# Attention and two expert layers on one core: values of two neighbouring head pairs in one group of matmuls

## The chip, the cores and the metric

The kernel runs on one core of a Trainium2 chip. The metric is the time of one execution in microseconds (us) of device time, as the median of several runs. The core has a matmul engine (PE, TensorE), whose weight loads the profile lists apart (PEld), a vector engine (DVE), an activation engine (ACT), GpSimd (POOL), and queues that issue DMAs (SP above all). Each engine works through its own list of instructions in order and waits on semaphores of the others.

## The reference, cut to what matters

Attention over 4 batches, 8 heads, 576 positions and head size 64, with a bias that depends on the two positions; its output, as 2304 tokens of 512, goes through a two-layer network (w_in to 2048, w_out back), and then through one of eight experts for each token.

```python
scores = scale * np.matmul(q, k.transpose(0, 1, 3, 2)) + bias
attn = np.exp(scores - max); attn = attn / (sum + 1e-9)
out = np.matmul(attn, v)                      # the products of this change
x = out.transpose(0, 2, 1, 3).reshape(2304, 512)
h = x @ w_in; g = np.maximum(0.01 * h, h)     # x @ w_in is the filler of attention
x = g @ w_out                                 # and then the experts
```

## The kernel before, in words

The program has three parts. The first, `phase1`, makes the bias table, does attention, and beside it already multiplies attention's output by w_in. The second multiplies by w_out and chooses experts, the third is the experts. The change touches the first alone.

Attention goes through 4 batches `b`; each batch is cut by query rows into two halves, `hf` 0 with 256 rows and `hf` 1 with 320 (`HALVES`); in each half four head pairs `p` follow each other. One (b, hf, p) is a group, of two steps in the first half and three in the second; a step is one block of 128 query rows (64 for the last block of a batch) for both heads of the pair. In a step `n` the program emits, in this order: the transposes of the step's probabilities (`transposes`, PE tiles `pst` and `psx`, copied by DVE or ACT to `pth` and `ptt`), the scores of step n+2 (`scores`, tile `pss`, two PSUM banks in turn; DVE adds the bias and takes the minimum, line 421), exponentials (`exps`, ACT), the normalisation of step n+1, small jobs (splits of q and k, loads), and units of the filler.

Numbers are carried in two parts, high and low, so that most products are three matmuls. The filler (`Filler`, `up_units`, line 528, tile `psh`) is x times w_in for the half that was finished before: 16 units of 12 matmuls each. `Filler.run(ns)` adds to a debt and hands out units while it is positive; `quota` is what a step adds, one half of it in the middle of the step and one at its end. Step 7 drains the filler.

At the last step of a group `values` multiplies the transposed probabilities of all its rows by the values: ten matmuls, two heads side by side in the columns of the array (each writes 64 of the 128 output partitions), five blocks of positions, into one bank `psv` of the pool `psM`, which the filler's `psh` shares and which has two banks. The profile counts each of these ten as two. In the next step `x_split` (through `values_out`) lets DVE copy the bank to x's high part (a CAST, line 78) and form the low part (line 82). After the fourth pair of a half, x times w_in of that half is added to the filler.

The order in which instructions stand on an engine isn't the order of this code: a scheduler places them, each engine's list being fixed when the program is built. The lines `tile_position=(0, 64 * h)` make the array work as two column tiles in `values`; scores, transposes and the filler use it whole.

## Time and profile before

| | us |
|---|---|
| median of three runs | 1012.41 (1012.28 to 1012.85) |
| the profiled execution, own time | 1009.6 |
| its span, first to last instruction | 1007.7 |
| PE busy in the span | 971.8 |
| DVE busy | 676.5 |
| ACT busy | 546.6 |
| matmuls of `values` begin, first and last | 60.0 and 504.2 |

The profiled execution is one run; what lies between its span and its own time is start and end outside the instructions. Attention with its filler ends at about 505 us, the last filler units at about 533 us. Busy PE includes the time in which a matmul's modelled end overlaps the next start, so starts are more telling than busy shares.

### The profile page before, as it was taken

The numbers are of one execution on the slowest core, as the hardware profiler recorded it, in microseconds if no ns is written. First come the engines' busy times: TensorE is split into PE (matmuls) and PEld (weight loads), VectorE is DVE, ScalarE is ACT, GpSimd is POOL, SyncE is SP. The second block draws the span as 40 slices with busy tenths as digits, with TensorE's granted clock in tenths as the row PEclk, the third lists the DMA queues.
The fourth block names the chain that finished last, engine by engine and source line by source line (L and its number), as shares of the span: only waits on it lengthen the run. The fifth ranks groups of instructions, "written<-read, shape, count | busy, mean of one in ns | idle before, by whom it ended". The sixth has DMA issues, their size and how long they took to land.

```text
span 1007.7 us, 19031 instructions
## 1 busy us (share of the span) xinstructions
PE 971.8 (96%) x6294; PEld 804.4 (80%) x6294; DVE 676.5 (67%) x1712; ACT 546.6 (54%) x1102; POOL 76.8 (8%) x85
## 2 busy tenths in 40 slices
PE   5999999999999999999998999999999999999996
PEld 2455878888899889998897888888877888888884
DVE  8999999889855677668676866579893355313312
ACT  6799787556756676656454333343562455424422
POOL 0023230000000000000000000001001111111110
PEclk9999999999999999999999999999999999999998
DMA  7898898999754576546187433437405257312410
GB/s 239 259 274 258 271 314 288 308 298 292 238 158 137 170 226 187 160 121 177 54 282 218 145 106 113 128 105 256 121 21 220 73 203 257 122 46 95 161 43 24
DMA packets 137600, 180.62 MB, mean 179 GB/s; under 512 B 19841, under 2 KB 89857, under 8 KB 137362
## 3 DMA queue, kind: packets, MB, share of 16 engines
q1 hardware_dynamic: 115554, 149.83, 48.5%
q10 hardware_dynamic: 18576, 18.97, 5.3%
q0 software_dynamic: 3360, 10.49, 3.1%
q8 instruction: 52, 0.85, 0.4%
q14 instruction: 58, 0.48, 0.2%
HBM read 196.65 MB, written 43.94 MB: 239 GB/s over the span
## 4 chain that ended last, share of the span: by engine, by line
PE 60%; issue 19%; DMA 11%; DVE 5%; ACT 2%; POOL 1%; SPq 1%; POOLq 0%; ACTq 0%; DVEq 0%
PE psx L787 19%; PE psh L528 16%; PE pss L416 7%; PE psv L503 7%; PE pst L467 5%; DMA out_dram<-o,sidx 5%; DMA wo_raw<-in_w_out_dram 3%; PE psb L272 3%; DMA w_raw<-in_w_in_dram 1%; POOL xg L1244 1%; DVE prob L421 1%; PE psx L489 1%; DMA prob<-bias 1%; DMA kraw<-in_k_dram 1%; DVE mk L230 1%
## 5 line engine op out<-in xcount | busy, mean ns | idle before, releaser
L528 PE MATMUL psh<-x,wi 128*128 128x256 f32 (+1 forms) x1536 | 224.7, 297 | 0.0
L528 PEld LDWEIGHTS psh<-x,wi 128*128 128x128 f32 x1536 | 211.0, 189 | 0.6 <-issue 0.5
L429 ACT ACTIVATE prob<-prob,stat 128x576 f32<-128x576 f32 x144 | 111.3, 773 | 66.4 <-DVE stat L421 56.8
L421 DVE CUSTOM_DVE_ANT_0 prob<-pss,prob 128x576 f32<-128x576 f32 x144 | 108.0, 751 | 20.4 <-PE pss L416 15.8
L787 PE MATMUL psx<-woh,gh 128*128 128x512 f32 x288 | 112.9, 392 | 0.0
L787 PE MATMUL psx<-wol,gh 128*128 128x512 f32 x288 | 112.6, 391 | 0.0
L787 PE MATMUL psx<-woh,gl 128*128 128x512 f32 x288 | 112.3, 390 | 0.0
L82 DVE TENSOR_TENSOR htl<-pt,hth 128x512 fp32r<-128x512 f32 x40 | 25.8, 686 | 124.8 <-ACT hth L70 124.0
L70 ACT ACTIVATE gh<-g 128x512 fp32r<-128x512 f32 x72 | 45.3, 631 | 112.7 <-PE psx L787 91.7
L467 PE MATMUL pst<-ident,prob 128*128 128x128 f32 x576 | 88.7, 278 | 4.3 <-DVE pth L78 2.1
L467 PEld LDWEIGHTS pst<-ident,prob 128*128 128x128 f32 x576 | 65.5, 140 | 24.4 <-issue 12.5
L416 PE MATMUL pss<-kt,qhi 128*128 128x288 f32 x256 | 81.0, 332 | 0.9 <-DVE kt L82 0.5
L416 PE MATMUL pss<-kt,qlo 128*128 128x288 f32 x256 | 72.3, 297 | 0.0
L503 PE MATMUL psv<-pth,vs 128*64 128x256 f32 (+1 forms) x512 | 71.6, 412 | 0.0
L1244 POOL DMA_INDIRECT xg<-x,gidx x22 | 23.4, 1063 | 615.2 <-DMA ws<-in_mw_dram 545.8
L804 DVE SCALAR_TENSOR_TENSOR junk<-x1s,en 128x512 bf16<-128x512 f32 x96 | 66.0, 688 | 1.1
L82 DVE TENSOR_TENSOR gl<-g,gh 128x512 fp32r<-128x512 f32 x72 | 49.3, 688 | 24.7 <-ACT gh L70 21.5
L1275 PE MATMUL pu<-w1h,xh 128*128 128x512 f32 x160 | 65.0, 406 | 0.3 <-ACT xh L70 0.3
L272 PE MATMUL psb<-mk,coef 128*32 128x79 f32 (+48 forms) x640 | 54.0, 411 | 11.6 <-DVE mk L230 9.8
L1275 PE MATMUL pu<-w1l,xh 128*128 128x512 f32 x160 | 63.3, 396 | 0.0
L1306 PE MATMUL pd<-w2h,hth 128*128 128x512 f32 x160 | 62.6, 391 | 0.7 <-ACT hth L70 0.7
L1275 PE MATMUL pu<-w1h,xl 128*128 128x512 f32 x160 | 63.3, 396 | 0.0
(223 smaller groups left out, 1833.5 us busy)
## 6 DMA issues: line engine op xcount, KB each, us to landing
ws<-in_mw_dram SPq DMA_DIRECT2D x164, 512.0 KB
prob<-bias SPq DMA_DIRECT2D x64, 288.0 KB
g<-h SPq DMA_DIRECT2D x72, 256.0 KB
prob<-bias SPq DMA_DIRECT2D x64, 256.0 KB
bias<-bt SPq DMA_DIRECT2D x36, 295.5 KB
h<-hst ACTq DMA_DIRECT2D x64, 160.0 KB
w_raw<-in_w_in_dram SPq DMA_DIRECT2D x16, 512.0 KB
h<-hst ACTq DMA_DIRECT2D x64, 128.0 KB
```

The lines of the kernel that those rows point to most:

```text
L82: nc.vector.tensor_tensor(out=out, in0=x, in1=hi.bitcast(F32), op=ALU.subtract)
L272: nc.tensor.matmul(ps[32 * q:32 * q + 32, :b - a], lhsT=e.coef.rearrange("p g h -> p (g h)"), rhs=x, start=True, stop=True, tile_position= ...
L416: nc.tensor.matmul(ps[:, jh, :288], lhsT=lhsT, rhs=kt[:, c0 + 288 * jh:][:, :288], start=(k == 0), stop=(k == len(ops) - 1),)
L421: nc.vector.tensor_tensor_reduce(out=prv, in0=ps[:, :, :288], in1=prv, scale=-0.125, scalar=3.0e38, op0=ALU.add, op1=ALU.min, accum_out=st ...
L429: nc.scalar.activation(out=pr[:, h], in_=pr[:, h], func=AF.Exp, bias=stat[:, 0, h:h + 1], scale=-1.0, accum_out=stat[:, 1, h:h + 1],)
L467: nc.tensor.transpose(ps[:, 128 * c:128 * c + 128], pr[:, h, 64 * h + 128 * c:][:, :128], e.ident)
L503: nc.tensor.matmul(ps[64 * h:64 * h + 64, :n], lhsT=vs[:, c, h], rhs=ph[:, h, c, :n] if c < 4 else pt[:, :n], start=(c == 0), stop=(c == 4 ...
L528: nc.tensor.matmul(ps[:, :n], lhsT=w[:, kc], rhs=x[:, kc, :n], start=(k == 0), stop=(k == 3 * KD - 1),)
L787: nc.tensor.matmul(ps, lhsT=a[:, c % 4], rhs=w[:, c], start=(k == 0), stop=(k == 3 * KF - 1))
L804: nc.vector.scalar_tensor_tensor(out=junk, in0=x1, scalar=1.0, in1=e.en[:, k], op0=ALU.mult, op1=ALU.mult, accum_out=e.dots[:, t, k:k + 1],)
L1275: nc.tensor.matmul(ps, lhsT=a[:, k], rhs=w[:, k, c], start=(i == 0), stop=(i == 3 * KD - 1))
L1306: nc.tensor.matmul(ps, lhsT=a[:, k], rhs=w[:, k], start=(k == 0 and j == 0), stop=(k == 7 and j == 2))
```

## The change

The products of pairs 0 and 1 are made together at the last step of pair 1, and those of pairs 2 and 3 at the last step of pair 3: 20 matmuls in a row where there were two times ten. For that the transposed probabilities of a pair are kept until its neighbour's are there (`pth` and `ptt` get two buffers, `pts` collects them). In the first half both results (2 x 256 columns) go to one PSUM bank, and `x_split` copies both with one CAST and one subtraction of 512 columns; in the second (320 columns) each has a bank, so that both banks of `psM` are taken for a while. `quota` grows by the estimated time `pv` of one pair's values for each pair, spread over the steps, and `fl.debt -= pv` takes as much away at the step in which a joined group stands; at step 8, three quarters of one for the group of the drained step 7. Over a half, what is added and what is taken are equal (2 `pv`).

```diff
--- before.py
+++ after.py
@@ -301,7 +301,7 @@
         self.nc, self.e = nc, e
         self.kv, self.v, self.qs, self.prob, self.ps = {}, {}, {}, {}, {}
         self.raw, self.qraw = {}, {}
-        self.pt = None
+        self.pt, self.pts = None, []
         self.free = list(range(PROBS))
         self.slot = {}
 
@@ -452,9 +452,10 @@
     def new_group(self):
         e = self.e
         self.pt = (
-            e.ptp.tile([128, 2, 4, 320], F32, tag="pth", name="pth", bufs=1),
-            e.ptp.tile([128, 320], F32, tag="ptt", name="ptt", bufs=1),
+            e.ptp.tile([128, 2, 4, 320], F32, tag="pth", name="pth", bufs=2),
+            e.ptp.tile([128, 320], F32, tag="ptt", name="ptt", bufs=2),
         )
+        self.pts.append(self.pt)
 
     def transposes(self, st, h):
         nc, e = self.nc, self.e
@@ -492,25 +493,38 @@
 
 
     def values(self, g):
+
         nc, e = self.nc, self.e
         b, hf, p = g
         n = HALVES[hf][1]
-        vs = self.v[b, p]
-        ph, pt = self.pt
-        self.psv = ps = e.psM.tile([128, 512], F32, tag="m", name="psv")
-        for c in range(5):
-            for h in range(2):
-                nc.tensor.matmul(
-                    ps[64 * h:64 * h + 64, :n], lhsT=vs[:, c, h], rhs=ph[:, h, c, :n] if c < 4 else pt[:, :n],
-                    start=(c == 0), stop=(c == 4), tile_position=(0, 64 * h),
-                )
+        tile = lambda: e.psM.tile([128, 512], F32, tag="m", name="psv")
+        if hf == 0:
+            self.psbank = ps = tile()
+            self.psv = [ps[:, n * k:n * k + n] for k in range(2)]
+        else:
+            self.psv = [tile()[:, :n] for k in range(2)]
+        for k, (ph, pt) in enumerate(self.pts):
+            vs = self.v[b, p - 1 + k]
+            for c in range(5):
+                for h in range(2):
+                    nc.tensor.matmul(
+                        self.psv[k][64 * h:64 * h + 64], lhsT=vs[:, c, h],
+                        rhs=ph[:, h, c, :n] if c < 4 else pt[:, :n],
+                        start=(c == 0), stop=(c == 4), tile_position=(0, 64 * h),
+                    )
+        self.pts = []
 
     def x_split(self, g, xh, xl):
         nc = self.nc
         b, hf, p = g
         n = HALVES[hf][1]
-        COPY[X_HI[b]](nc, xh[:, p, :n], self.psv[:, :n])
-        lo_dve(nc, xl[:, p, :n], self.psv[:, :n], xh[:, p, :n])
+        if hf == 0:
+            parts = [(slice(p - 1, p + 1), self.psbank[:, :2 * n].rearrange("p (k i) -> p k i", k=2))]
+        else:
+            parts = [(p - 1 + k, self.psv[k]) for k in range(2)]
+        for q, ps in parts:
+            COPY[X_HI[b]](nc, xh[:, q, :n], ps)
+            lo_dve(nc, xl[:, q, :n], ps, xh[:, q, :n])
 
 
 def up_units(nc, e, b, hf, xh, xl):
@@ -652,7 +666,7 @@
         if prev is None:
             return
         pb, ph, pp = prev
-        if pp == 0:
+        if pp == 1:
             pool = e.xp if ph == 0 else e.late
             xs = [pool.tile([128, KD, HALVES[ph][1]], F32R, tag=f"x{i}{ph}", name=f"x{i}", bufs=1) for i in range(2)]
         at.x_split(prev, *xs)
@@ -667,6 +681,8 @@
         last = st[3] == HALVES[hf][2][-1]
 
         quota = 40 * 800.0 / 6.5 if n < 8 else KF * 1600.0 / 8 if hf == 0 else (13 if b == 0 else 17) * 1280.0 / 12
+        pv = 20 * HALVES[hf][1] if n >= 8 else 0.0
+        quota += 2 * pv / (8 if hf == 0 else 12)
         nx = steps[n + 2] if n + 2 < ns else None
         while loaded < ns and at.free:
             at.load_bias(steps[loaded])
@@ -693,6 +709,10 @@
         if n == 7:
             fl.drain()
         else:
+            if last and p % 2:
+                fl.debt -= pv
+            if n == 8:
+                fl.debt -= 0.75 * pv
             fl.run(quota / 2)
         if nx and nx[3] != 4:
             at.exps(nx, 1)
@@ -703,8 +723,9 @@
                 e.late = ctx.enter_context(tc.tile_pool(name="late", bufs=1, side="left"))
                 e.wi.append(new_w_in(e.late))
                 at.free.append(PROBS)
-            at.values(g)
-            prev = g
+            if p % 2:
+                at.values(g)
+                prev = g
     at.x_split(prev, *xs)
     fl.add(up_units(nc, e, prev[0], prev[1], *xs))
     return fl
```

How the lists of instructions move, at three places. PE, second half of the third batch, first head pair, before: the last filler matmuls, ten matmuls of values, then the next step's transposes and scores.

```order
L528 MATMUL psh<-x_4047,wi_77 128x256
L528 MATMUL psh<-x_4046,wi_78 128x256
L503 MATMUL psv<-pth,vs 64x320 x8
L503 MATMUL psv<-ptt,vs 64x320 x2
L467 MATMUL pst<-ident,prob 128x128 x4
L489 MATMUL psx<-ident,prob 128x128
L416 MATMUL pss<-kt,qtail 128x288 x8
L467 MATMUL pst<-ident,prob 128x128 x4
L528 MATMUL psh<-x_4046,wi_77 128x256
```

After, the same half with pairs 0 and 1:

```order
L416 MATMUL pss<-kt,qhi 128x288
L416 MATMUL pss<-kt,qlo 128x288
L510 MATMUL psv<-pth,vs 64x320 x8
L510 MATMUL psv<-ptt,vs 64x320 x2
L510 MATMUL psv<-pth,vs 64x320 x8
L510 MATMUL psv<-ptt,vs 64x320 x2
L468 MATMUL pst<-ident,prob 128x128 x4
L490 MATMUL psx<-ident,prob 128x128
L416 MATMUL pss<-kt,qtail 128x288 x8
L468 MATMUL pst<-ident,prob 128x128 x8
L416 MATMUL pss<-kt,qhi 128x288
```

Two groups have become one without anything between them; the filler no longer follows the next step's second transposes but comes later, and the transposes of two steps stand together.

DVE at the same places, from the normalisation (line 445) to the reduction of scores (line 421), before:

```order
L445 TENSOR_SCALAR prob<-prob,stat 128x576
L78 CAST x_4755<-psv 128x320
L78 COPY pth<-pst 128x4x128
L82 TENSOR_TENSOR x_4756<-psv,x_4755 128x320
L78 COPY ptt<-psx 128x128
L421 ISA prob,stat<-pss,prob 128x576
```

After:

```order
L445 TENSOR_SCALAR prob<-prob,stat 128x576
L78 CAST x_4937<-psv 128x320
L82 TENSOR_TENSOR x_4938<-psv,x_4937 128x320
L78 CAST x_4937<-psv 128x320
L78 COPY pth<-pst 128x4x128
L82 TENSOR_TENSOR x_4938<-psv,x_4937 128x320
L78 COPY ptt<-psx 128x128
L421 ISA prob,stat<-pss,prob 128x576
```

The first pair's CAST and subtraction stand ahead of the second pair's CAST, and that ahead of the copy of transposed probabilities (`pth`).

PE, first half of the first batch, pairs 2 and 3 (step 7), after:

```order
L416 MATMUL pss<-kt,qlo 128x288
L510 MATMUL psv<-pth,vs 64x256 x2
L468 MATMUL pst<-ident,prob 128x128 x4
L416 MATMUL pss<-kt,qhi 128x288
L416 MATMUL pss<-kt,qlo 128x288
L416 MATMUL pss<-kt,qhi 128x288
L416 MATMUL pss<-kt,qlo 128x288
L510 MATMUL psv<-pth,vs 64x256
L510 MATMUL psv<-ptt,vs 64x256 x2
L510 MATMUL psv<-pth,vs 64x256 x8
L510 MATMUL psv<-ptt,vs 64x256 x2
L468 MATMUL pst<-ident,prob 128x128 x4
```

Here the scheduler has put other work into the joined group: two matmuls and the last thirteen stand in these rows in two pieces, and one and four more stand in two pieces ahead of them; the other fifteen joined groups are whole.

## Rows read from the trace of the kernel before

**Rows 1.** Windows: stretches of the span; busy us of each engine, TensorE clock, DMA share, GB/s.

```profile
0.00:107.00 107.00, 93.50 (x921) 50.59 (x922) 97.18 (x242) 86.73 (x181) 18.83 (x27) 1.00 0.84 255
107.00:148.00 41.00, 39.80 (x310) 33.89 (x309) 37.42 (x93) 32.37 (x85) 13.04 (x15) 1.00 0.96 306
148.00:246.00 98.00, 92.87 (x698) 84.09 (x699) 86.48 (x216) 60.26 (x136) 1.48 (x1) 1.00 0.92 298
246.00:504.60 258.60, 257.91 (x1995) 229.59 (x1993) 181.78 (x507) 159.60 (x355) 0.00 (x0) 1.00 0.55 165
```

**Rows 2.** Chain of waits, shares by line, of 148 to 246 us, then 246 to 504.6.

```profile
by line: DMA wo_raw<-in_w_out_dram 34.9%; PE psh L528 9.1%; DMA w_raw<-in_w_in_dram 5.7%; issue 5.1%; PE pss L416 4.9%; DVE wo_t L107 4.8%; DVE prob L421 4.8%; DVE wo_t L103 4.2%; PE pst L467 3.4%; DMA prob<-bias 3.2%; PE psv L503 2.9%; DVE
...
by line: PE psh L528 43.8%; PE psv L503 18.1%; PE pss L416 17.2%; PE pst L467 14.2%; PE psx L489 1.7%; DMA prob<-bias 1.2%; issue 0.8%; ACT prob L429 0.7%; ACT kt L70 0.5%; PE psx L485 0.5%; ACT pth L70 0.4%; DVE prob L421 0.3%; DVE pth L78
```

**Rows 3.** Timeline of PE, 270 to 300 us: start us, us, operation, count.

```profile
286.40 1.92 PE L528 MATMUL psh<-x,wi 128*128 128x320 f32 x12
288.16 0.60 PE L467 MATMUL pst<-ident,prob 128*128 128x128 f32 x4
...
289.13 1.92 PE L528 MATMUL psh<-x,wi 128*128 128x320 f32 x12
290.98 1.95 PE L503 MATMUL psv<-pth,vs 128*64 128x256 f32 x16
...
293.29 0.65 PE L467 MATMUL pst<-ident,prob 128*128 128x128 f32 x4
293.78 0.27 PE L489 MATMUL psx<-ident,prob 128*128 128x128 f32 x1
...
294.03 0.30 PE L416 MATMUL pss<-kt,qlo 128*128 128x288 f32 x1
294.16 0.30 PE L416 MATMUL pss<-kt,qhi 128*128 128x288 f32 x1
```

**Rows 4.** Timeline of PE at 291.4 and at 292.3 us, inside one group of values.

```profile
291.25 0.60 PE L503 MATMUL psv<-pth,vs 128*64 128x256 f32 x4
...
291.90 0.81 PE L503 MATMUL psv<-pth,vs 128*64 128x256 f32 x5
```

**Rows 5.** Windows of tile psv alone (count is after the x), before and after 250 us.

```profile
0.00:250.00 250.00, 38.92 (x280) 21.72 (x280) 11.81 (x27) 1.00 0.89 280
250.00:504.60 254.60, 48.12 (x360) 24.25 (x360) 16.06 (x36) 1.00 0.55 163
```

**Rows 6.** Timeline of PE, 86.5 to 102.5 us: a group of values in two pieces.

```profile
87.45 0.65 PE L503 MATMUL psv<-pth,vs 128*64 128x256 f32 x2
...
89.43 1.72 PE L503 MATMUL psv<-pth,vs 128*64 128x256 f32 x13
```

**Rows 7.** Timeline of PE, 200 to 203.2 us: a group that takes longer.

```profile
200.44 2.09 PE L503 MATMUL psv<-pth,vs 128*64 128x256 f32 x15
...
203.11 0.33 PE L467 MATMUL pst<-ident,prob 128*128 128x128 f32 x1
```

**Rows 8.** Waits of DVE, 148 to 246 us: us in total, times, longest.

```profile
DVE wo_t L99 <- DMA wo_raw<-in_w_out_dram: 7.6, 8, 1.8
```

**Rows 9.** Waits of DVE, 246 to 504.6 us.

```profile
DVE x L78 <- PE psv L503: 11.2, 13, 1.5
```

**Rows 10.** Timeline of DVE, 293 to 296 us, behind one group of values.

```profile
293.41 0.42 DVE L78 CAST x<-psv 128x256 fp32r<-128x256 f32 x1 [1.45 <-PE psv L503]
293.98 0.69 DVE L78 COPY pth<-pst 128x512 f32<-128x512 f32 x1 [0.15 <-PE pst L467]
294.59 0.41 DVE L82 TENSOR_TENSOR x<-psv,x 128x256 fp32r<-128x256 f32 x1
294.92 0.28 DVE L78 COPY ptt<-psx 128x128 f32<-128x128 f32 x1
295.12 0.75 DVE L421 CUSTOM_DVE_ANT_0 prob<-pss,prob 128x576 f32<-128x576 f32 x1
```

**Rows 11.** Groups of DVE instructions, shapes kept apart: out x count, busy, mean ns.

```profile
L78 DVE CAST x<-psv 128x320 fp32r<-128x320 f32 x16 | 7.8, 487 | 5.2 <-PE psv L503 5.2
```


## The prediction

> **What bounds the kernel now.** I read the windows first, then the chain of waits stretch by stretch, then the timeline of PE around one group of values, then the waits of DVE. Groups of values run from 60 to 504 us, and that part falls into three. From 246 to 504.6 us PE is busy 257.91 of 258.6 us at the full clock [rows 1], and the chain there is nearly all PE, 18.1% of it the matmuls of values [rows 2]: each nanosecond that PE saves is a nanosecond of the kernel. From 148 to 246 us it is another kernel: PE is idle 98 - 92.87 = 5.1 us, DVE is busy 86.48 of 98 us, DMA 92% [rows 1], and the chain's largest share is the load of raw w_out, 34.9%, with its conversion on DVE (wo_t) behind it [rows 2]. A saving of PE may sink into a wait there. Before 148 us the bias and the conversion of w_in stand beside attention, DVE and DMA are about as full as PE [rows 1]. The reader is to see that the same saving has another worth in each stretch.
>
> **Step 1, entries and exits of groups.** A group of values works the array as two column tiles, its neighbours use it whole. With 256 columns, twelve filler matmuls and the step to a transpose take 288.16 - 286.40 = 1.76 us; the same twelve and the step to values 290.98 - 289.13 = 1.85 us [rows 3]. The entry costs 0.09 us. From the first matmul of values to the next transpose it is 293.29 - 290.98 = 2.31 us [rows 3]. Inside, the second pair of matmuls starts at 291.25 and the fifth at 291.90 [rows 4], so a pair takes 0.65/3 = 0.217 us and ten pairs 2.17 us: 0.14 us more go to the first pair (291.25 - 290.98 = 0.27, 0.05 too many) and the exit (0.09). Together 0.09 + 0.14 = 0.23 us for each time that PE goes to values and back.
>
> How often: 280 + 360 = 640 matmuls, 20 of them a group, are 32 groups [rows 5]; two were in two pieces, as the one at 87.45 and 89.43 [rows 6] and one like it, which makes 34 times. After the change there are 16 groups, one of them in four pieces by the order of instructions: 19 times. The change saves 15 x 0.23 = 3.45 us of PE. Of these, 18 groups after 250 us [rows 5] become nine, so 9 x 0.23 = 2.1 us fall where PE is the bound and count in full. Six, 1.4 us, fall before 250 us, where they are worth between nothing and all; I count half, 0.7: three of them stand before 148 us, where PE is 93.5 of 107 and 39.8 of 41 us busy [rows 1], three where PE has only about a fifth of the chain [rows 2].
>
> That the seam inside a joined group costs nothing is not shown by any row. The nearest is a pair inside a group, where going on to other weights and other probabilities costs 0.217 us and no more [rows 4]. Against it stands that the seam also changes the output: the 0.05 us that the first pair takes too long could belong to a new output instead of the array's change, and then each seam pays it again, 15 x 0.18 = 2.7 us. I take 3.45, after the nearest rows; 2.7 lies within the range. The Trainium skill, TensorEngine Tiling (Array Packing), Key Properties, says that a change of tiling mode drains TensorE, and a change of tile alone doesn't. By that rule the seam is free and the sum is the 3.45 us of [rows 3, 4]; no row of the kernel before shows a seam.
>
> **Step 2, waits inside a group.** The group at 200.44 us takes 203.11 - 200.44 = 2.67 us [rows 7] where the one of [rows 3] takes 2.31: 0.36 us. I read it as a wait for the last transposed probabilities, which are copied just before. There are three more of these between 184 and 249 us, none dearer, some 1.1 us for the four. In a joined group the older pair's ten matmuls go first, over 2 us, and cover such a copy. All four lie in the stretch where DVE and DMA also bind; half counts, 0.6 us, with 0 and 1.1 as bounds.
>
> **Step 3, DVE.** In the first halves two CASTs of 0.42 us and two subtractions of 0.41 us [rows 10] become one of each at 512 columns. At 320 columns a CAST takes 0.487 us [rows 11], 0.067 more for 64 columns, so 512 should take 0.42 + 4 x 0.067 = 0.69 us, an estimate. A pair of groups saves 2 x (0.42 + 0.41) - 2 x 0.69 = 0.3 us of DVE, eight times. In the PE-bound stretch that is worth nothing, as DVE is idle 77 of 258.6 us [rows 1]; from 148 to 246 us two such pairs stand, 0.6 us at best. I count nothing.
>
> **Step 4, what a long group does to its neighbours.** PE hands DVE no new scores during a group. Already DVE waits for values at the head of its list, 11.2 us over 13 of the 18 groups after 246 us, up to 1.5 us [rows 9], with the copy of the next transposes queued behind [rows 10]. A joined group lasts ten pairs longer, 2.2 us with 256 columns and a quarter more with 320, and the filler pauses behind it, so PE comes to the next transposes sooner than it did. I followed the order of a second half with the durations of [rows 10, 11]. DVE, from 0.12 us after the first transpose's start: second CAST 0.49, copy 0.61 until the next start, second subtraction like the CAST 0.49, small copy 0.20, reduction 0.75, a split of q like the small copy 0.28, copy of the next step's transposes 0.69; that is done at 3.6 us. PE needs that bank after eight scores, eight transposes, three scores, a small transpose and four scores. Four transposes take 293.78 - 293.29 = 0.49 us, the second score stands 0.74 us after the first transpose, each further one 0.13 us later [rows 3]: eight scores are over at 1.65, the transposes at 2.6, the rest at about 3.7 us. So hardly anything to spare and nothing lost; in the first halves the margin is a few tenths better, since only the first of these copies stands in the way. I put 0.06 us on each of eight joined groups of second halves, 0.5 us in all; the bounds are 0 and 0.5 us a group, 4 us (an estimate, from the 0.49 of the CAST that newly stands ahead of the copy).
>
> **What costs nothing.** The filler's units are the same in number and in work; what the quota adds in a half is what the joined groups take away. Its cover is the PE-bound stretch itself: the units are only moved within a half. The loads of values (vs) move on SP's queue behind the joined group; they are used a half later, and the bias loads behind them wait for later transposes than that group anyway. Two banks held by values in a second half would stop the filler, but no unit is due until both have been read. The ACT list carries the same work.
>
> **Sum.** -2.1 - 0.7 - 0.6 + 0.5 = -2.9 us. It is made against the profiled execution, whose own time is 1009.6 us and span 1007.7 us, so 1006.7 us for such a one; the median of the runs stands 2.8 us above it, and 2.9 us off the median of 1012.41 is 1009.5 us.
>
> **Rivals.** (a) The early savings sink: steps 1 and 2 are worth nothing before 250 us, and the joined groups cost 0.15 us of wait each, 16 x 0.15 = 2.4 us, against the 2.1 us saved later. For it: DMA 92% busy and DVE waiting 7.6 us for raw w_out [rows 8]. Result +0.3, 1012.7 us.
>
> (b) The change doesn't do what it says: each seam costs what entry and exit did, and only step 2's share is left, 0 to 1 us, 1011.9 us. The even pairs of [rows 4] speak against it.
>
> (c) Slower, by a starved DVE in 148 to 246 us. Four joined groups stand there, each withholding scores for 2.2 us or more. DVE has 98 - 86.5 = 11.5 us to spare, of which 7.6 go to waits for raw w_out [rows 1, 8], so 3.9 us can be absorbed; what the groups add beyond that lengthens the stretch. If DVE finds nothing to do for 2.5 us in each of four, 10 - 3.9 = 6.1 us are lost, less the 2.1 us saved later: +4.0, 1016.4 us. It decides from about 6 us of added DVE waits in that stretch on. For it: in each list, work behind the CAST can't pass it. Against: the filler that used to stand behind groups now stands before them, and the wo_t conversions lie in between.
>
> (d) More than forecast: the new order also removes half of PE's 5.1 idle us in 148 to 246 us, and steps 1 and 2 count in full: -3.5 - 1.1 - 2.6 = -7.2, 1005.2 us. Nothing in the order says that it should.
>
> **How the numbers follow.** Forecast 0.48, (d) 0.12, (a) 0.22, (b) 0.05, (c) 0.13. A measurement of this kernel can tell about 0.2%, 2.0 us, from no change: its three runs lie within 0.06%. Forecast and (d) are faster, 0.60; (a) and (b) the same, 0.27; (c) slower, 0.13. The range reaches from (d), 1005.0 us, to 1013.5 us: (a) with step 4 at 0.25 us a group, -2.1 + 4.0 = +1.9, falls a little beyond, and most of (c) is left out, about 0.15 together with what lies below. The forecast's own range is 1007.9 to 1010.4 us, from all of step 1 counted and step 4 at nothing to the dearer seam with step 4 at 1 us.
>
> **What would show it.** Twenty values matmuls with 256 columns between their first start and the next transpose in about 2 x 2.17 + 0.14 = 4.5 us [rows 3, 4]; if it is 4.55 or more, the seam pays. From 246 us to the end of attention about 2 us less. PE waiting for pth or ptt behind joined groups, up to 0.5 us each, would be step 4. The number of CASTs of x falls from 32 to 24. The forecast is wrong if the stretch from 148 to 246 us changes by more than 2 us either way, or if DVE's wait for values, 11.2 us, grows by more than 10 us and PE shows waits to match.

## The result, and the profile after

| | kernel before | changed kernel |
|---|---|---|
| median of runs, side by side | 1012.35 us (6 runs) | 1022.27 us (6 runs) |
| ratio | 1 | 1.0115, 95% interval 1.0089 to 1.0141 |
| profiled execution, own time / span | 1009.6 / 1007.7 us | 1021.72 / 1019.9 us |

The change makes the kernel slower by 9.9 us, about 1.2%. The forecast was 2.9 us faster, the range ended at 1013.5.

Where the time went is read from windows whose ends stand at the same points of the program in both kernels: just behind the last values of batch 0's first half, of batch 0, of batch 1, and of all attention. First the kernel before, then the changed one (columns as in [rows 1]: span, then busy time of PE, PEld, DVE, ACT and POOL with counts, PE's granted clock, DMA share, GB/s).

```profile
0.00:102.00 102.00, 88.50 (x879) 45.60 (x879) 92.24 (x232) 82.76 (x172) 16.92 (x25) 1.00 0.85 257
102.00:160.10 58.10, 55.12 (x431) 47.37 (x430) 53.68 (x130) 46.07 (x116) 16.42 (x18) 1.00 0.91 287
160.10:278.60 118.50, 114.81 (x871) 103.01 (x869) 102.26 (x263) 74.02 (x165) 0.00 (x0) 1.00 0.89 286
278.60:504.60 226.00, 225.65 (x1747) 202.18 (x1745) 154.67 (x432) 136.11 (x302) 0.00 (x0) 1.00 0.52 154
```

```profile
0.00:103.70 103.70, 86.89 (x874) 44.59 (x874) 92.59 (x230) 83.18 (x172) 18.08 (x25) 0.98 0.83 254
103.70:165.40 61.70, 57.49 (x437) 48.42 (x436) 52.73 (x129) 47.46 (x118) 15.61 (x18) 1.00 0.90 273
165.40:291.10 125.70, 117.54 (x883) 105.66 (x881) 102.37 (x260) 74.72 (x164) 0.00 (x0) 0.97 0.84 270
291.10:514.70 223.60, 222.93 (x1735) 201.61 (x1733) 153.19 (x423) 135.42 (x300) 0.00 (x0) 1.00 0.51 154
```

The four stages change by +1.7, +3.6, +7.2 and -2.4 us, +10.1 in all; the other 2 us of the 12.1 between the two profiled executions lie behind attention. In the third stage PE does 12 matmuls more (883 for 871), one unit of the filler that the new quota brings forward; it is missing in the fourth (1735 for 1747). Twelve take 1.76 us with 320 columns [rows 3] and less with 256, say 1.4 us. Without that the third stage loses about 5.8 us and the fourth gains about 1.0. PE's idle time in the third grows from 118.50 - 114.81 = 3.7 to 125.70 - 117.54 = 8.2 us, and its mean clock falls to 0.97. DVE does the same 102 us of work in either.

In the first stage, 1.1 of the 1.7 us are lost before the first matmul of scores (it starts at 30.93 us before and at 32.01 us after), while PE still builds the bias table. No group of values has run by then, so a joined group can't be what costs them.

The part of the prediction that counted entries and exits holds. This is PE's timeline at one joined group of a first half (start us, us, operation, count):

```profile
311.71 1.95 PE L510 MATMUL psv<-pth,vs 128*64 128x256 f32 x16
313.49 0.60 PE L510 MATMUL psv<-ptt,vs 128*64 128x256 f32 x4
313.92 1.90 PE L510 MATMUL psv<-pth,vs 128*64 128x256 f32 x16
315.65 0.60 PE L510 MATMUL psv<-ptt,vs 128*64 128x256 f32 x4
316.18 0.65 PE L468 MATMUL pst<-ident,prob 128*128 128x128 f32 x4
```

The first pair's twenty matmuls take 313.92 - 311.71 = 2.21 us, the second's with the exit 316.18 - 313.92 = 2.26, together 4.47 us. The limit for a dear seam was 4.55: the seam costs nothing that shows. Two separate groups took 2 x 2.31 and one more entry [rows 3].

What is new lies behind the joined groups. Waits of PE in the third stage, of the kernel before (one row) and of the changed one (waited for: us in total, times, longest):

```profile
PE pst L467 <- DVE pth L78: 2.1, 2, 1.5
```

```profile
PE pst L468 <- DVE pth L78: 7.1, 4, 3.1
PE psx L490 <- ACT pth L70: 0.8, 2, 0.4
PE pst L468 <- DVE prob L445: 0.3, 1, 0.3
```

PE waits 7.1 us for copies of transposed probabilities. The longest of these waits, on PE (the last rows of the joined group and what follows):

```profile
254.53 0.71 PE L510 MATMUL psv<-ptt,vs 128*64 128x320 f32 x4
255.17 0.65 PE L468 MATMUL pst<-ident,prob 128*128 128x128 f32 x4
...
255.69 1.31 PE L416 MATMUL pss<-kt,qtail 128*128 128x288 f32 x8
256.83 0.29 PE L416 MATMUL pss<-kt,qhi 128*128 128x288 f32 x1
260.25 0.66 PE L468 MATMUL pst<-ident,prob 128*128 128x128 f32 x4 [3.12 <-DVE pth L78]
...
262.94 0.63 PE L542 MATMUL psh<-x,wi 128*128 128x256 f32 x2
```

and the same time on DVE (the idle time before an instruction in brackets, with what ended it):

```profile
254.30 0.49 DVE L82 TENSOR_TENSOR x<-psv,x 128x320 fp32r<-128x320 f32 x1
257.31 0.43 DVE L99 TENSOR_SCALAR wo_t<-wo_raw 128x512 uint32<-128x512 uint32 x1 [2.52 <-DMA wo_raw<-in_w_out_dram]
257.77 0.69 DVE L103 SCALAR_TENSOR_TENSOR wo_t<-wo_raw,wo_t 128x512 uint32<-128x512 uint32 x1
258.50 0.69 DVE L107 SCALAR_TENSOR_TENSOR wo_t<-wo_raw,wo_t 128x512 uint32<-128x512 uint32 x1
259.11 0.48 DVE L78 CAST x<-psv 128x320 fp32r<-128x320 f32 x1
259.51 0.68 DVE L78 COPY pth<-pst 128x512 f32<-128x512 f32 x1
```

The transposes of 255.17 could be copied from about 255.7 us on. DVE reaches their copy at 259.51, since a conversion of w_out stands before it in the list and waits 2.52 us for its load, then takes 1.8 us, and the second CAST of the joined group follows. PE needs the bank at 257.1 and stands still for 3.1 us; no unit of the filler comes between the group and 262.94. Behind the group at 159.86 us it is the same picture with 2.2 us. Behind the one at 189.32 a late copy costs 1.6 us; DVE's wait for raw w_out (2.25 us) ended at 190.63 there, and the conversions of two tiles stand between it and the copy. That wait isn't clearly new: the kernel before has a wait of 1.5 us for such a copy too, up to 197.56 us.

The loss is uneven. From the end of pair 1 in batch 0's second half to the end of pair 1 in batch 1's, and from there to the end of batch 1, first the kernel before, then the changed one:

```profile
129.42:248.60 119.18, 113.29 (x857) 101.48 (x856) 105.55 (x263) 76.72 (x177) 8.21 (x8) 1.00 0.93 300
248.60:278.60 30.00, 29.66 (x234) 25.54 (x231) 24.50 (x68) 21.66 (x49) 0.00 (x0) 1.00 0.76 235
```

```profile
133.13:255.20 122.07, 114.07 (x857) 101.25 (x857) 105.60 (x260) 79.65 (x179) 7.97 (x8) 0.99 0.88 285
255.20:291.10 35.90, 32.34 (x245) 28.55 (x243) 25.89 (x67) 21.32 (x47) 0.00 (x0) 0.95 0.72 216
```

Up to the end of the group that starts at 249.63 us, with the same 857 matmuls, the change loses 2.9 us over 119. Behind that one group it loses 5.9 us more, 4.5 without the filler's unit: the wait of 3.1 us, and the low clock after it (last section).

### The profile page after: what moved, and what is told of

The parts are those of the page before. It is cut to its first block, busy times and chain, and to the rows that moved or that the text cites. A ratio compares the mean times of both kernels' runs of the same rounds, so it can differ in the third digit from the quotient of the medians.

```text
span 1019.9 us, 18991 instructions
## 1 busy us (share of the span) xinstructions
PE 974.3 (96%) x6294; PEld 807.7 (79%) x6294; DVE 674.4 (66%) x1696; ACT 548.8 (54%) x1102; POOL 77.1 (8%) x85
## 4 chain that ended last, share of the span: by engine, by line
PE 48%; DMA 19%; issue 18%; DVE 10%; ACT 3%; SPq 1%; POOL 1%; ACTq 0%; POOLq 0%; DVEq 0%
PE psx L808 19%; PE psh L542 11%; DMA out_dram<-o,sidx 7%; PE pss L416 5%; PE psv L510 5%; PE pst L468 4%; DMA wo_raw<-in_w_out_dram 3%; DMA w_raw<-in_w_in_dram 2%; PE psb L272 2%; DMA kraw<-in_k_dram 2%; DMA prob<-bias 1%; DVE prob L421 1%; DMA qraw<-in_q_dram 1%; DVE mk L230 1%; DMA w_t<-wo 1%
## 5 line engine op out<-in xcount | busy, mean ns | idle before, releaser
L70 ACT ACTIVATE pth<-pst 128x512 f32<-128x512 f32 (+1 forms) x100 | 54.6, 549 | 37.7 <-PE pst L468 33.1
L416 PE MATMUL pss<-kt,qlo 128*128 128x288 f32 x256 | 74.6, 304 | 0.0
L808 PEld LDWEIGHTS psx<-woh,gl 128*128 128x128 f32 x288 | 54.5, 189 | 11.3
## 6 DMA issues: line engine op xcount, KB each, us to landing
g<-h SPq DMA_DIRECT2D x72, 256.0 KB
prob<-bias SPq DMA_DIRECT2D x64, 256.0 KB
```

What stands on the lines that cost most here:

```text
L70: nc.scalar.activation(out=out, in_=in_, func=AF.Copy)
L416: nc.tensor.matmul(ps[:, jh, :288], lhsT=lhsT, rhs=kt[:, c0 + 288 * jh:][:, :288], start=(k == 0), stop=(k == len(ops) - 1),)
L808: nc.tensor.matmul(ps, lhsT=a[:, c % 4], rhs=w[:, c], start=(k == 0), stop=(k == 3 * KF - 1))
```

## The experiments

My first theory (T1): behind a joined group the filler, given up there, no longer covers PE while DVE is held by conversions that wait for raw w_out. The rivals were: joining itself does it (T2, and rival (c) of the prediction as its mechanism), the moved filler alone does it (T3), the late groups lose too (T4). T5 to T7 came later and are stated where they are tried. All ratios below are to the kernel before, run beside, with 95% intervals.

**1 and 2: the filler's terms alone, and joining alone.** e1 is the change without these lines, e2 the kernel before with them:

```diff
+        pv = 20 * HALVES[hf][1] if n >= 8 else 0.0
+        quota += 2 * pv / (8 if hf == 0 else 12)
...
+            if last and p % 2:
+                fl.debt -= pv
+            if n == 8:
+                fl.debt -= 0.75 * pv
```

> Joined groups as in the change, but the filler's quota and debt as before, so that the filler also runs behind a joined group. Theory T1 (PE idles behind joined groups because the filler that covered the late copies of probabilities is given up there): most of the loss goes, 1010 to 1014 us, the PE stalls over 1.5 us at 169, 197 and 260 us and the drops of the clock there are gone. T2 (joining itself puts loads and conversions into a worse order on SP and DVE, whatever the filler does): still 1019 to 1023 us. T3 (moving the filler is bad by itself): 1010 to 1012 us, so T1 and T3 are told apart by the next kernel.

> The kernel before with the change's quota and debt alone, groups separate. T3 (moving the filler is bad by itself): 1018 to 1024 us. T1 (it needs both, the long group that keeps scores from DVE and the missing filler behind it): a part of the loss, 1012 to 1016 us. T2: 1012 to 1013 us, as the kernel before.

Measured: e1 1021.05 us, ratio 1.0072 (1.0058 to 1.0086); e2 1016.99 us, 1.0042 (1.0026 to 1.0058). The first is T2's number. T1 as stated falls: with the filler back behind the groups PE still waits 6.9 us for copies by DVE between 100 and 285 us, and DVE waits more for raw w_out than in the change (15.3 us against 10.1). T3 falls as the whole cause: the filler's terms cost 4 us with separate groups, a little more than T1 expected there, but the joined groups lose with them and without. With separate groups and these terms PE waits 4.7 us for copies by DVE between 60 and 300 us, against 2.1 in the kernel before, so in this build moving the filler alone already lengthens these waits.

**3: joined in batches 2 and 3 only**, the filler's terms with it.

```diff
+    def joined(self, b, hf):
+        return b >= 2
...
-            if p % 2:
+            if p % 2 or not at.joined(b, hf):
                 at.values(g)
```

> The whole change, quota and debt too, but only in the batches 2 and 3 (from about 278 us on); separate groups and the old quota in batches 0 and 1. T1 and T2 both place the loss before about 262 us: here 1009.5 to 1011.5 us, since seven or eight joined groups at 0.23 us save about 1.8 us and nothing else changes before 278 us. A theory T4 that joined groups of second halves cost by their two banks or by the copies behind them in the PE-bound stretch too: 1012.5 us or more.

Measured: 1010.20 us, 0.9972 (0.9953 to 0.9990): faster than the kernel before. T4 falls; the loss is made before 280 us.

**4: raw w_out loaded two half steps earlier.**

```diff
     nc.sync.dma_start(out=raw, in_=e.w_out[r])
     yield
+    yield
+    yield
```

> The change, with the load of each raw w_out tile issued two half steps earlier than its conversion (two more yields between them), so that DVE should hardly wait for it. If the long stalls behind joined groups come from DVE held by that wait (T1 with the raw load as what holds it), the waits for wo_raw fall from 10.1 us to under 3 us, the stalls at 169 and 260 us and their clock drops go: 1014 to 1017 us. If the conversions' own work or the missing filler alone is enough for the stalls, 1019 to 1022 us.

Measured: 1019.04 us, 1.0061 (1.0038 to 1.0083). The edit didn't do what it should: DVE's waits for raw w_out between 100 and 285 us are 11.5 us, not under 3, since the loads stay where they were: 162.2 to 251.2 us, against 161.9 to 251.1 in the change. The stalls stayed (7.7 us for copies by DVE). The clock stayed at 1.00 up to 500 us in this one, worth some of the 3 us.

**5 and 6: w_out from step 44 instead of 20**, in the change and in the kernel before.

```diff
-        spread(20 + 2 * c, 0, lambda c=c: w_out_narrow(nc, e, c), 1)
+        spread(44 + 2 * c, 0, lambda c=c: w_out_narrow(nc, e, c), 1)
```

> The change, with the load and conversion of w_out begun at step 44 instead of step 20, so that it lies in the PE-bound stretch (about 300 to 490 us) and not beside the attention of batch 1. If joining costs in 160 to 280 us because w_out's loads and conversions leave DVE and the DMA engines no slack there (T1 and rival (c) of the prediction), the stalls of PE over 1 us between 165 and 290 us and their clock drops go, and this kernel stands within 3 us of its own control with separate groups. If joining costs by itself (PE's long group, whatever else DVE does), it stays 7 to 11 us above that control.

> The control: the kernel before with the same move of w_out to step 44. If w_out bounds the stretch from 160 to 280 us, it is faster than the kernel before there by 3 to 5 us and 1007 to 1012 us in all; if w_out's waits there only take the place of others, 1012 to 1016 us.

Measured: e5 1018.46 us, 1.0056 (1.0035 to 1.0077); e6 1013.28 us, 1.0013 (0.9997 to 1.0028). Neither expectation was put to a test: the scheduler pulled the loads and conversions back beside batch 1 (162 to 261 us in e5, 160 to 250 in e6), where DVE still waits 11.4 and 6.7 us for raw w_out. The pair counts only as two more builds, joined 5 us behind separate.

**7: the CAST written later.**

```diff
         at.transposes(st, 0)
-        values_out()
...
+        values_out()
         side(n, 1)
         at.done(st)
```

> The change, with the CAST and the subtraction of x written behind the second transposes of the next step, not between its first transposes and its tail. If PE stalls behind joined groups because the CAST, held until the long group ends, stands ahead of the copy of the next transposes on DVE, the waits of PE for pth copied by DVE fall from 7.1 us to under 3 us between 100 and 285 us: 1015 to 1018 us. If DVE is late for another reason (no scores during the group, conversions), 1020 to 1024 us.

Measured: 1018.05 us, 1.0069 (1.0039 to 1.0099); PE's waits for copies by DVE between 100 and 285 us fall from 7.1 to 5.0 us. That lies between the two expectations: the CAST ahead of the copy is a part of it, not the whole.

**8 and 9: two buffers for vs.** New theory T5: SP's queue waits at a load of vs (the values of a pair) for the joined group, and other loads stand behind.

```diff
-        vs = e.kvp.tile([128, 5, 2, D], F32, tag=f"vs{p}", name="vs", bufs=1)
+        vs = e.kvp.tile([128, 5, 2, D], F32, tag=f"vs{p}", name="vs", bufs=2)
```

> The change, with two buffers for each tile of values vs, so that the load of the next batch's values need not wait for a joined group. Theory T5: SP waits at the head of its queue for the joined group before it may load vs (7.0 us over 5 times between 60 and 300 us, 2.1 us before the change), the loads of raw w_out, raw w_in, q and the bias stand behind, and DVE, which is held by those, lets PE wait. Then SP's waits for psv go, the stalls of PE in the second halves of batches 0 and 1 come back to about those of the kernel before, 1012 to 1016 us. If PE's long group itself takes the work from DVE (rival (c) of the prediction), SP's waits go and the time stays at 1018 to 1023 us.

> The control: the kernel before with two buffers of vs. It waited only 2.1 us for vs between 60 and 300 us: 1010 to 1013 us by either theory.

Measured: e8 1019.83 us, 1.0088 (1.0062 to 1.0114); e9 1017.03 us, 1.0046 (1.0026 to 1.0066). In e8 SP still waits 6.9 us for values between 60 and 300 us, because the scheduler put the loads further ahead on SP's list, where they wait again; T5 was not tested by it. The surprise is the control: separate groups, nothing changed but a buffer, and 5 us slower than the kernel before. With it the scheduler laid out the lists of all engines anew from the start, and the layout alone can cost this much (T6: the loss is a worse layout by chance). Where e9 loses tells it from the joined groups, though: in its profiled execution it is 3.5 us behind at the end of the first stage and 2.8 us more behind attention, but batch 1 takes 118.6 us, as in the kernel before (118.5).

**10 and 11: joined in first halves only, in second halves only** (`return hf == 0`, `return hf == 1`).

> The change in first halves alone (two steps a pair, one bank), quota and debt with it; second halves as before. No load of vs stands behind a joined group here, since the values of the next batch are loaded in second halves. T5: no loss, 1011 to 1013 us. Rival (c): four joined groups before 230 us cost half of what the eight did, 1015 to 1018 us.

> The change in second halves alone. T5: the whole loss, 1018 to 1023 us. Rival (c): half of it, 1015 to 1018 us.

Measured: e10 1018.51 us, 1.0077 (1.0048 to 1.0106); e11 1016.73 us, 1.0052 (1.0031 to 1.0072). T5 falls as the whole cause. First halves alone lose too, and PE's longest wait for a copy by DVE there, 2.5 us up to 196.1 us, stands where SP issues no load of vs (none between 166 and 237 us). In the change itself, the load of raw w_out behind the longest wait was issued at 251.09 us, ahead of the loads of vs at 253.04. SP does wait for values in both, 5.5 and 5.1 us; what that costs in second halves wasn't separated. Each half costs a part, 6.4 and 4.7 us over the runs of the kernel before beside them, 11.1 together beside the change's 9.9.

**12 and 13: the conversions left out.** T7: a joined group costs where DVE and the DMA engines have no slack to catch up.

```diff
 def w_in_split(nc, e, f):
+    if f:
...
+        hi, lo = w_in_columns(e, f)
+        t = e.w0.rearrange("p (k n) -> p k n", k=KD)
+        COPY[WIN_HI[f // 4]](nc, hi, t)
+        LO[WIN_LO[f // 4]](nc, lo, t, hi)
+        return
...
 def w_out_narrow(nc, e, c):
-    nc.sync.dma_start(out=raw, in_=e.w_out[r])
-    yield from convert_f64(nc, raw, t)
-    nc.sync.dma_start(out=e.wo_d[r], in_=t)
+    nc.sync.dma_start(out=e.wo_d[r], in_=e.w0)
```

> The change, leaving out the loads and the conversions of w_in and w_out but for the first of w_in, whose result stands in for all others (wrong weights; splits, stores and filler stay). That takes some 16 MB of loads and 90 conversions off DVE and the DMA engines before 290 us. Theory T7: a joined group costs where DVE and the DMA engines have no slack, because the copies, loads and scores it holds up for 2.2 us more cannot be caught up; with slack it saves its switching as in the late stretch. Then this kernel is 1 to 4 us faster than its control with separate groups. Theory T6 (the scheduler's lists are worse by chance in every kernel that changes the early part): it is still 4 to 8 us slower than the control.

> The control: the kernel before with the same loads and conversions left out. By either theory 10 to 25 us faster than the kernel before, since PE's stalls before 290 us and part of the bias stage's waits go.

Measured: e12 1026.47 us, 1.0140 (1.0115 to 1.0165); e13 1024.06 us, 1.0122 (1.0099 to 1.0145). Wrong weights send tokens to other experts behind attention, so these times say nothing beside the kernel before; the pair does, and best up to the end of attention. Windows at the points of the program used above, e12 joined, then e13 separate:

```profile
0.00:102.80 102.80, 86.43 (x875) 43.56 (x875) 86.54 (x218) 84.56 (x175) 17.78 (x26) 1.00 0.84 256
102.80:161.00 58.20, 56.30 (x435) 48.07 (x434) 38.63 (x97) 47.44 (x118) 13.98 (x18) 1.00 0.75 224
161.00:275.90 114.90, 113.82 (x883) 102.69 (x882) 78.04 (x210) 73.80 (x162) 0.00 (x0) 1.00 0.61 187
275.90:499.40 223.50, 222.88 (x1733) 201.58 (x1733) 153.14 (x423) 135.54 (x300) 0.00 (x0) 1.00 0.51 154
```

```profile
0.00:101.40 101.40, 86.84 (x881) 44.98 (x881) 86.23 (x222) 84.38 (x175) 17.27 (x26) 1.00 0.84 258
101.40:157.90 56.50, 54.53 (x430) 47.17 (x429) 38.46 (x97) 47.04 (x117) 13.66 (x18) 1.00 0.81 246
157.90:271.00 113.10, 112.50 (x870) 100.65 (x869) 77.27 (x211) 71.87 (x160) 0.00 (x0) 1.00 0.61 180
271.00:497.20 226.20, 225.86 (x1747) 202.28 (x1745) 154.70 (x432) 136.19 (x302) 0.00 (x0) 1.00 0.52 154
```

With DVE at 77 of 113 us instead of 102 of 118, and DMA at 0.61 instead of 0.89, joining costs 114.9 - 113.1 = 1.8 us in the third stage, of which 1.4 are the filler's unit, where it cost 7.2. In this pair of builds the joined groups of that stage cost next to nothing, now that DVE and DMA have slack. In the second stage it is 1.7 for 3.6, and in the first, where the bias is made and little of the conversions had stood, 1.4 for 1.7: there the loss stays, 0.4 of the 1.4 again before the first scores. Over all e12 is 2.4 us behind its control, so T7's number (1 to 4 us faster) was missed, but T6's (4 to 8 slower) too; and the control's attention ends only 7.4 us before that of the kernel before, less than the 10 expected. The edit takes away two things at once, the load on DVE and the DMA engines and the conversions that stand ahead of a copy; which of them counts it can't say. Nor does it test T5: SP waits 13.8 us for values between 60 and 285 us here, 13.3 in the control, but the loads of raw w_out that would stand behind are left out.

**14 and 15: raw w_out loaded by POOL's queue** (`nc.gpsimd.dma_start` for `nc.sync.dma_start`).

> The change, with the loads of raw w_out issued by POOL instead of SP, so that they don't stand behind loads of bias that wait for PE's transposes behind a joined group. If DVE is held by raw w_out because of that order on SP, DVE's waits for wo_raw fall from 10.1 us to under 5 us and the time to 1015 to 1018 us. If the DMA engines themselves are full, or DVE's backlog alone does it, 1018 to 1023 us.

> The control: the kernel before with the loads of raw w_out issued by POOL: 1009 to 1014 us by either theory.

Measured: e14 1030.74 us, 1.0181 (1.0155 to 1.0207); e15 1031.92 us, 1.0197 (1.0169 to 1.0225). The means cost more than what it should measure: the control alone loses 19 us, and DVE waits 15.0 and 10.5 us for raw w_out. Nothing follows on the order of SP's loads.

**16 to 18: the same work put beside the late groups.** The kernel of experiment 3 (e18 is that kernel again) and the kernel before, with w_out converted a second time (e16, e17):

```diff
         spread(20 + 2 * c, 0, lambda c=c: w_out_narrow(nc, e, c), 1)
+    for c in range(KF):
+        spread(46 + 2 * c, 0, lambda c=c: w_out_narrow(nc, e, c), 1)
```

> Joined groups in batches 2 and 3 only, as in the third kernel, and w_out's loads and conversions done a second time from 280 us on, so that the late stretch gets the work that stands beside batch 1. T7 (a joined group costs where DVE and the DMA engines have no slack): the 2.3 us that joined groups saved between the end of batch 1 and the end of attention turn into a loss, 1 to 8 us against its control, with PE stalls of over 1 us at the next transposes. T6 (only a worse placement of the early part): the saving of about 2 us stays.

> The control: the kernel before with w_out's loads and conversions done a second time from 280 us on. Its stretch from 278 us to the end of attention grows by 2 to 8 us; what counts is the difference to the joined one.

> The third kernel again, beside the doubled pair on the same chip: joined groups in batches 2 and 3 alone, without the doubled work. T6 and T7 both: 2 to 3 us faster than the kernel before, the ratio 0.9972 again within its interval.

Measured: e18 1009.58 us, 0.9964 (0.9941 to 0.9987), the gain of e3 again; e16 1019.70 us, 1.0076 (1.0049 to 1.0104); e17 1020.41 us, 1.0076 (1.0049 to 1.0103): the gain is gone. Windows of batch 2 and of batch 3, e16 joined, then e17 separate:

```profile
282.80:404.90 122.10, 117.11 (x897) 105.53 (x894) 95.00 (x247) 74.42 (x165) 0.00 (x0) 0.99 0.79 252
404.90:514.20 109.30, 109.30 (x853) 99.00 (x852) 76.52 (x215) 61.42 (x139) 0.00 (x0) 1.00 0.44 130
```

```profile
281.40:400.90 119.50, 116.80 (x884) 104.08 (x880) 94.99 (x250) 72.95 (x164) 0.00 (x0) 0.99 0.80 253
400.90:512.60 111.70, 111.70 (x867) 100.08 (x865) 77.36 (x220) 62.26 (x141) 0.00 (x0) 1.00 0.45 131
```

Twelve of the sixteen doubled conversions end up beside batch 2, four already beside batch 1. Beside batch 2 the joined kernel is 122.1 - 119.5 = 2.6 us slower, 1.4 of it a filler's unit done earlier, and PE's idle time is 5.0 us against 2.7. Beside batch 3, at half the DMA share, it is 2.4 us faster, 1.4 of it that unit. For e18 and the kernel before, with equal counts of matmuls, the same stretch shows the plain gain: 223.7 us against the 226.0 above.

```profile
279.80:503.50 223.70, 223.60 (x1747) 203.11 (x1745) 153.88 (x424) 136.16 (x302) 0.00 (x0) 1.00 0.52 156
```

So over both batches a gain of 2.3 us has become 231.4 - 231.2 = 0.2 us of loss, and beside batch 2, where the conversions stand, about 1.2 us of loss. The sign is T7's, but the size is below the 1 to 8 us expected, and it isn't clear of the layout: batch 1, where both have separate groups and the same work, takes 121.8 us in e16 and 119.5 in e17, 2.3 us apart. By the medians e16 and e17 differ by 0.7 us the other way, within their intervals. That the gain is gone is measured; that a loss took its place is not shown. The control's stretch grew by 231.2 - 226.0 = 5.2 us, as expected.

## Why the prediction was wrong, point by point

**What bounds the kernel.** The three stretches, and that a saving has another worth in each, were right. That early work could cost more than it saves was left to rival (c).

**Step 1.** Right in its mechanism and in its late part. The seam is free, and batches 2 and 3 alone give 2.3 us in the profile (e18) and 2.5 to 2.9 us by the medians (e18, e3), where 2.1 us after 250 us were forecast. That half of the early 1.4 us would be seen was wrong; nothing of them is.

**Step 2.** Right: the waits inside groups are gone. Every joined group that stands in one piece takes 4.46 or 4.47 us up to the next instruction with 256 columns and 5.53 or 5.54 with 320, early ones as late ones, where four early groups of the kernel before took 0.1 to 0.4 us too long. The saving is drowned by what happens behind the groups.

**Step 3.** Right: 24 CASTs for 32, a wide one 693 ns at most (0.69 us forecast), and no use of it.

**Step 4 is the step that failed.** It put 0.06 us on eight joined groups of second halves, with 0.5 us a group as the bound, and said of first halves that "the margin is a few tenths better". Behind four of the joined groups before 262 us PE waited 1.5 (for a copy by ACT), 2.2, 1.6 and 3.1 us, the 1.6 in a first half; its waits for copies by DVE in the third stage grew from 2.1 to 7.1 us in all. The list of DVE that I followed came from a late group and held DVE's own copies; the lists of the early groups also hold conversions that wait for raw w_out or follow it, 1.8 us of work each and up to 2.5 us of wait. What the low clock adds behind such a wait, about 1.65 us a time, stood in no term either.

**"What costs nothing" failed with it**: "Its cover is the PE-bound stretch itself" holds after 290 us only. The filler's terms alone cost 4 us (e2). The loads of vs, which I counted at nothing too, do wait longer on SP (7.0 us against 2.1), but the load behind the longest stall was issued ahead of them, and e10 loses without one near its longest wait.

**Rival (c), at 0.13, had the sign, but its rule was not met in its stretch.** It asked for about 6 us of added DVE waits from 148 to 246 us. In the windows that hold this stretch (129.42 to 248.60 us before, 133.13 to 255.20 after) DVE's idle time grew from 119.18 - 105.55 = 13.6 to 122.07 - 105.60 = 16.5 us, by 2.8, and the time by 2.9. Only with what follows the fourth of its groups does it come to more: in the third stage DVE's idle time grew from 118.50 - 102.26 = 16.2 to 125.70 - 102.37 = 23.3 us (a longer stage with the same work brings that by itself). Its mechanism, DVE with nothing to do for lack of scores, is a part at most. In the third stage, first before and then after, DVE's wait for scores grew by 1.8 us, and its largest wait, for raw w_out, from 7.6 to 10.1:

```profile
DVE prob L421 <- PE pss L416: 0.5, 2, 0.3
```

```profile
DVE wo_t L99 <- DMA wo_raw<-in_w_out_dram: 10.1, 7, 2.5
...
DVE prob L421 <- PE pss L416: 2.3, 3, 1.1
```

Where PE waits longest, the scores are not what is missing: DVE stands at a conversion and comes late to a copy. And (c) stopped at 246 us, before the dearest wait; the loss begins before 103 us and ends at 291.

**The sum.** The late part was forecast at -2.1 and came as about -1.0 in the change itself after batch 1; 0.3 us of what is missing are idle time of PE (0.67 against 0.35), the rest wasn't traced. From the end of pair 1 in batch 1's second half to the end of attention (256.0 us before, 259.5 after) it is 3.5 us more, where the prediction's sign was about 2 less from 246 us on. The early part, -1.3 us from steps 1 and 2, came as 1.7 + 3.6 + 7.2 - 1.4 = +11.1.

**What stays open.** Six builds with all groups joined (the change, e1, e4, e5, e7, e8) lie at 1.0056 to 1.0115, their mean 1.0077; four with separate groups (the kernel before, e2, e6, e9) at 1 to 1.0046, mean 1.0025. Joining costs about 0.5% by that, some 5 us, of the 9.9.

The stage of batch 1 separates them better than the whole time. Between the same points of the program, each kernel's one profiled execution takes there, less an estimated 1.4 us for each unit of the filler more (plus 1.4 for each fewer) by the count of PE's matmuls:

| groups in batch 1 | us |
|---|---|
| separate: kernel before, e6, e9, e3, e18 | 118.5, 116.9, 118.6, 119.2, 119.5 |
| separate, with four doubled conversions: e16, e17 | 121.8, 119.5 |
| separate, with the filler's terms: e2 | 121.6 |
| joined, without the filler's terms: e1 | 122.2 |
| joined in first halves, in second halves: e10, e11 | 120.9, 122.3 |
| all joined: the change, e4, e5, e7, e8 | 124.3, 121.9, 125.5, 119.5, 123.5 |

The last two of the first row are one and the same kernel. The means of the first and the last row, 118.5 and 122.9, are 4.4 us apart, and the rows only touch: the lowest of the last is e7, where the CAST is written later. So most of the 5.8 us that the change loses in this stage comes with joining and its filler's terms, not with one unlucky layout. Either alone costs 3 to 4 us (e2, e1, one build each), so the two don't add up. In batch 0's second half the rows lie closer: 58.1 to 59.0 us in the first, 59.6 to 61.7 in the last. The table also says how far e12 and e13 carry: with all conversions in place e7 is only 1.0 us above the mean of the first row, so one pair at 0.4 us makes T7 likely and doesn't prove it.

Open remain the 1.1 us before the first scores and the 2 us behind attention, which e9, with separate groups, shows as well (2.6 and 2.8 us); how the loss splits between DVE's full list, the full DMA queues and the conversion that happens to stand ahead of a copy; and the rest of the difference between the medians, in which the kernel before is the best of its kind that was run.

## What to carry to other kernels

Price a longer block on one engine in the stretch where the others have least slack, with the list that really stands behind it there, and not with the list of a quiet stretch: a conversion that waits for its load holds up the copy behind it as well as any other instruction. Where the gain is sure only in the stretch that the engine bounds, make the change only there: joined in batches 2 and 3 alone it is 0.28% and 0.36% faster in two measurements, and the best kernel found here. And where a scheduler lays out the program, run a control with an edit that should do nothing, and compare stages and not only the whole: here such an edit cost 0.46%, and by its profile none of that in the stage in question.

## What was not expected of the hardware

PE's clock fell to its lower level, 1.2 GHz, behind some of the new waits. Two of these stretches, and one behind attention that the kernel before doesn't have (a fourth, in the bias stage from about 22.8 to 26.4 us, shows in the 0.98 of the first stage; it alone would be enough for the 1.1 us lost before the first scores):

```profile
169.70:173.00 3.30, 3.30 (x17) 3.29 (x16) 2.62 (x7) 2.23 (x5) 0.00 (x0) 0.50 0.61 184
261.80:265.10 3.30, 3.30 (x17) 3.30 (x17) 3.22 (x10) 2.02 (x5) 0.00 (x0) 0.50 0.64 169
555.40:558.70 3.30, 3.30 (x10) 2.60 (x10) 0.80 (x2) 0.20 (x1) 0.00 (x0) 0.50 0.65 223
```

At half the clock 3.3 us hold 1.65 us of work at the full one, so each costs about that; the last is most of the 2 us lost behind attention. The first followed a wait of 2.16 us, the second one of 3.12, the third one of 2.46; the fourth stands behind shorter ones, of 1.69 and 0.58 us. But the length of the wait alone doesn't decide: in e4 a wait of 3.26 us was followed by the full clock, and so was one of 2.64 us in the kernel before.

```profile
259.71 0.66 PE L468 MATMUL pst<-ident,prob 128*128 128x128 f32 x4 [3.26 <-DVE pth L78]
```

```profile
545.06 0.38 PE L756 MATMUL pse<-ident,emb 8*128 8x8 f32 x4 [2.64 <-issue]
```

```profile
259.80:263.20 3.40, 3.40 (x28) 3.18 (x29) 3.38 (x11) 2.65 (x5) 0.00 (x0) 1.00 0.47 134
```

```profile
545.06:548.50 3.44, 3.44 (x18) 2.84 (x19) 1.79 (x3) 1.31 (x3) 0.00 (x0) 1.00 0.47 138
```

These are the wait in e4, that in the kernel before, and the windows behind the two, whose clock, third from the right, is 1.00. What does decide, these runs don't show.
